# Later batches read x once and move its turned blocks inside SBUF; the first batch's softmax maximum is taken in two parts

## The chip, the cores and the metric

One core of a Trainium2 chip runs the whole program. The metric is the device time of one execution in microseconds (us). The engines are named as in the profile: PE (TensorE matmul) with PEld (its weight loads), DVE (VectorE), ACT (ScalarE), POOL (GpSimd) and SP (SyncE), whose queue issues the DMAs here.

## What is computed

Two rounds of attention over a small set of 32 inducing rows, then an FFN with a squared ReLU over all 49,920 rows:

```python
B, N, m, C = 4, 12480, 32, 128          # x: B x N x C, inducing: m x C, all float32
def mab(q, kv):                          # softmax attention, scale 1/sqrt(C)
    s = scale * (q @ kv.transpose(0, 2, 1))
    s = s - s.max(-1, keepdims=True)
    a = np.exp(s)
    a /= a.sum(-1, keepdims=True) + 1e-09
    return a @ kv
h = mab(I, x)                            # I: the inducing rows, for each batch
y = mab(x, h).reshape(B * N, C)
hidden = np.maximum(y @ w_in, 0.0)       # w_in: 128 x 2048
out = hidden * hidden @ w_out            # w_out: 2048 x 128
```

## The kernel before, in words

**Tiles.** A batch of 12,480 rows is cut into 26 lanes of 480 rows (LANE = 32 x 15), and the lanes into NG = 7 groups: six of four lanes and one of two. A group is a tile `xn` in SBUF (partition p holds 15 rows of 128 numbers) and, turned, a tile `xt` (the 128 channels on the partitions). One FFN block works on one lane: 104 blocks in all, each with 16 hidden slices in four quads.

**Order.** The program builds a list of tasks with `add(engine, ns, fn, due, needs, ...)`: an engine, a cost in ns, a due time, the tasks that it needs and the buffers that it takes or reads. `Plan.run` schedules the list with these costs: of the tasks that an engine could start now it takes the one with the earliest due time, and the instructions are emitted in that order. Each engine, and SP's queue, then works through its own order on the chip and waits wherever an operand is not there yet. T_MAIN is the planned start of the FFN blocks, BLOCK = 15,100 ns is one block's share; the other constants at the top (W_DUE, FIRST_DUE, MIX_DUE, S1_LEAD, HI_DUE and so on) set due times.

**First attention of batch 0** (`FirstBatch`). Seven tiles `xn` are loaded. For each group PE transposes it in 128x128 pieces (L671), ACT or DVE copies the result to `xt` (L254, a helper), PE makes the scores `sp` (L696), and DVE writes the row maximum into a column of `bare` (L702). The scores of the first four groups are copied to SBUF. When all seven maxima are there, L569 to L585 form the common maximum over groups and lanes (`mx`, `lanes`, `top`, `neg`), ACT takes the exponentials (`e`, L603), DVE turns them (`et`, L610), and PE sums `et` with `xn` into `nb` (L619).

**End of a batch's first attention** (`first_end`). From the sums and totals come `hT` (the attended rows, turned; copied by L254) and `hw`, the product of `hT` with w_in in four chunks of 512 columns: PE `wp` (L753), ACT copies the chunk (L757), DVE writes the remainder on half of the partitions (L762). An FFN quad needs its chunk of `hw`.

**Second attention** (`Second`). For a group PE makes `na` from `xt` and `hT` (L796); DVE and ACT do a softmax over 32 in `d` (L802 to L826); the result is turned (`a`), split into a high and a low part (`sw`), and four DMAs a lane spread it to `st` (L843), the FFN's input. The first lane of the program has a small version of its own (`mini`, tiles with `0m`), which ends with L873 and L877 in place of the DMAs.

**Weights.** w_in and w_out arrive as pairs of words and are put together on ACT and DVE (`weights`, L287 to L308, joined at L353 and L372), in four chunks each.

**FFN block.** h on PE (L942), ReLU and square on ACT (L949, L963), `hi` and `lo` on DVE (L968, L973), three products each on PE (L1027, one slice by L1017); in the first two blocks one product instead (L984). The result is turned (`ob`, L1048) and stored by four DMAs (L1054).

**First attention of batches 1 to 3** (`First`), beside the FFN blocks of the batch before: SP loads the group as `xn` (L411), and once more from DRAM in blocks: `xb`, one buffer for two lanes, eight DMAs of 60 KB in runs of 128 bytes (L440). One DVE transpose of 32x32 blocks writes `xb` to `xt` (L443), twice for a full group, once for the half one. `weigh` then makes the scores (L465), maximum, exponentials and sums (L472 to L534), with a running maximum: each group's `neg` is the smaller of its own and the one before, and sums are scaled by `fade`.

Of the kernel before, what the change touches and what calls it, by code (L numbers as in the profile page):

```python
# [162 lines left out]
def induced_attention_then_squared_relu_ffn(  # L163
# [232 lines left out]
    class First:  # L396
# [3 lines left out]
        def __init__(self, b, g, due, begun=None):  # L400
# [19 lines left out]
            for h in range(self.L // 2):  # L420
                self.turned.append(self.turn_blocks(h, due - 6000 + 3000 * h))
# [7 lines left out]
        def turn_blocks(self, h, due):  # L429
            b = self.b  # L430
            bb = Buffer("xb")
            v = {}

            def load():
                v["xb"] = xb_pool.tile([P, 2, NR, S], F32, tag="xb", name=f"xb_{self.n}_{h}")
                for l in range(2):
                    at = self.at + (2 * h + l) * LANE
                    rows = x[b, at:at + LANE, :].rearrange("(t r) (g c) -> g t r c", r=NR, c=S)
                    for c in range(P // S):
                        nc.sync.dma_start(v["xb"][c * S:(c + 1) * S, l], rows[c])  # L440

            def turn():
                nc.vector.transpose(  # L443
                    self.xt_tile()[:, 2 * h:2 * h + 2].rearrange("c l r t -> c (l r t)"),
                    v["xb"].rearrange("p l r c -> p (l r c)"),
                )
# [103 lines left out]
    class FirstBatch:  # L550


        def __init__(self, due, step, mix_due, mix_step):
            self.s = s = state.setdefault(0, {"xt": {}, "bxt": {}, "turned": {}})
            s["first"] = self
            self.sp, self.xn, self.bsp = {}, {}, {}
            self.loaded, self.tops, bxs = [], [], []
            v = {}
# [3 lines left out]
            kept = NG - 3  # L562

            for g in range(NG):
                self.group(g, due + step * g, g < kept, bare)

            def lanes():
                v["mx"] = tiny.tile([P, 1], F32, tag="mx", name="mx_0")
                nc.vector.tensor_reduce(v["mx"], bare[:, 0, :NG], axis=AX.X, op=ALU.max)  # L569

            def lanes2():
                v["lanes"] = tiny.tile([P, Q], F32, tag="lanes", name="lanes_0")
                nc.vector.tensor_scalar_mul(v["lanes"], lane_q, v["mx"])

            def gather():
                v["tops"] = self.last_sp[:, LANE:LANE + Q]
                nc.tensor.matmul(v["tops"], same, v["lanes"], start=True, stop=True)

            def most():
                v["top"] = tiny.tile([P, 1], F32, tag="top", name="top_0")  # L580
                nc.vector.tensor_reduce(v["top"], v["tops"], axis=AX.X, op=ALU.max)

            def shift():
                self.neg = tiny.tile([P, 1], F32, tag="neg", name="neg_0", bufs=4)
                nc.vector.tensor_scalar_mul(self.neg, v["top"], -scale)  # L585

            d = mix_due
            bg = self.bsp[NG - 1]
            t = add("DVE", 100, lanes, d - 3000, self.tops)
            t = add("DVE", 110, lanes2, d - 3000, [t])  # L590
            t = add("PE", 110, gather, d - 3000, [t], reads=[bg])
            t = add("DVE", 100, most, d - 3000, [t], reads=[bg])
            shifted = add("DVE", 70, shift, d - 3000, [t])
            bn = Buffer("s")
            powered, mixed = None, None
            for g in range(NG):
# [4 lines left out]
                def power(g=g, R=R, c=c):  # L601
# [3 lines left out]
                        bias=self.neg[:R], scale=scale, accum_out=bare[:R, 1, g:g + 1],  # L605
# [8 lines left out]
                def mix(g=g, R=R, c=c):  # L614
                    if g == 0:
                        v["nb"] = early_bank("nb_0")[:, :C]
                    for r in range(NR):
# [525 lines left out]
```

## Time and profile before

| | before |
|---|---|
| median of three runs | 1653.51 us (1652.34 to 1654.84) |
| the profiled execution | 1653.15 us, span 1651.4 us |
| busy PE / DVE / ACT / POOL | 1615.4 / 1535.6 / 1526.3 / 45.1 us |
| granted TensorE clock, mean | 0.993 |
| DMA | 101.30 MB in 389,085 packets, 368,848 of them under 512 B |
| HBM read / written | 48.94 / 25.56 MB |

In a row of the timeline stand start (us), duration (us), engine, source line, operation, output and inputs with shapes; "xN" merges N neighbours; a bracket gives the idle time before it and what ended it. "SPq" is SP's queue. A row of a group of instructions has count, then busy us and the mean in ns, then idle time before and what ended most of it. A row of DMA issues has the KB of one and the median us from issue to landing. A row of waits has total us, times and the longest.

### The profile page before, as it was taken

What the parts mean: (1) busy time and instruction counts of PE and PEld (TensorE: products, weight loads), DVE (VectorE), ACT (ScalarE), POOL (GpSimd) and SP (SyncE); (2) the same over time, 40 slices, a digit from 0 to 9 for tenths busy, and PEclk for the clock granted to TensorE, in tenths of its full rate; (3) what the DMA queues carried; (4) which work ended last, traced back from release to release, by engine and by line L of the source; (5) the groups of instructions that cost most, each with busy time, mean ns of one, the idle gap of its engine ahead of it and who ended that gap; (6) DMA issues with size and microseconds to landing.
All of it is one profiled execution on the core that took longest, in us unless ns stands there. A gap on an engine that the chain in (4) does not pass through costs nothing.

```text
span 1651.4 us, 22141 instructions
## 1 busy us (share of the span) xinstructions
PE 1615.4 (98%) x8004; PEld 1282.1 (78%) x8004; DVE 1535.6 (93%) x1457; ACT 1526.3 (92%) x1425; POOL 45.1 (3%) x39
## 2 busy tenths in 40 slices
PE   7889999999999999999999999999999999999998
PEld 5368787887778788888877778878787878888886
DVE  6759999999989999999999999999999999999997
ACT  5679999999989999999989999999999999999997
POOL 0000000000000000000000000000000000000000
PEclk9999999999999999999999999999999999999999
DMA  7441533422243333323233334233012212111211
GB/s 246 111 87 43 100 56 69 70 44 60 49 86 71 59 68 79 57 49 77 41 63 78 76 60 91 47 67 73 13 31 43 40 24 51 37 31 19 43 30 19
DMA packets 389085, 101.30 MB, mean 61 GB/s; under 512 B 368848, under 2 KB 385136, under 8 KB 388976
## 3 DMA queue, kind: packets, MB, share of 16 engines
q1 hardware_dynamic: 388976, 99.89, 29.8%
q8 instruction: 63, 1.03, 0.3%
q14 instruction: 46, 0.38, 0.1%
HBM read 48.94 MB, written 25.56 MB: 45 GB/s over the span
## 4 chain that ended last, share of the span: by engine, by line
PE 89%; DVE 5%; SPq 2%; issue 2%; DMA 1%; ACT 1%; DVEq 0%; POOL 0%; ACTq 0%
PE op L1027 57%; PE h L942 21%; PE op L1017 5%; DVE lo L973 2%; SPq L440 1%; PE nb L518 1%; PE na L796 1%; DVE hi L968 1%; PE sp L465 1%; PE op L984 1%; PE xtp L671 1%; SPq L843 1%; PE wp L753 1%; DVE hw L762 0%; DMA st<-sw 0%
## 5 line engine op out<-in xcount | busy, mean ns | idle before, releaser
L949 ACT ACTIVATE g<-h 128x960 f32<-128x960 f32 x832 | 780.4, 983 | 63.8 <-PE h L942 46.5
L973 DVE TENSOR_TENSOR lo<-g,hi 128x1920 fp32r<-128x1920 f32 (+1 forms) x409 | 823.7, 2015 | 15.2 <-DVE z L823 0.3
L963 ACT ACTIVATE g<-g 128x1920 f32<-128x1920 f32 (+1 forms) x419 | 760.2, 1814 | 4.5
L942 PE MATMUL h<-st,hw 128*128 128x480 f32 x1664 | 516.0, 392 | 6.4 <-DMA st<-sw 5.1
L968 DVE CAST hi<-g 128x1920 fp32r<-128x1920 f32 (+1 forms) x409 | 442.6, 1082 | 47.7 <-ACT g L963 39.7
L1027 PE MATMUL op<-hi,wo_hi 128*128 128x480 f32 x1530 | 442.5, 403 | 0.0
L1027 PE MATMUL op<-hi,wo_lo 128*128 128x480 f32 x1530 | 435.7, 383 | 0.0
L1027 PE MATMUL op<-lo,wo_hi 128*128 128x480 f32 x1530 | 415.4, 381 | 0.6 <-DVE lo L973 0.6
L942 PEld LDWEIGHTS h<-st,hw 128*128 128x128 f32 x1664 | 309.0, 188 | 93.9 <-issue 28.2
L1027 PEld LDWEIGHTS op<-hi,wo_hi 128*128 128x128 f32 x1530 | 286.2, 188 | 81.4 <-issue 36.6
L1027 PEld LDWEIGHTS op<-lo,wo_hi 128*128 128x128 f32 x1530 | 286.6, 188 | 54.8 <-issue 5.9
L1027 PEld LDWEIGHTS op<-hi,wo_lo 128*128 128x128 f32 x1530 | 287.2, 188 | 49.1 <-issue 3.0
L1017 PE MATMUL op<-g,wo_whole 128*128 128x480 f32 x204 | 98.9, 566 | 0.0
L820 POOL TENSOR_SCALAR z<-z 128x15 f32<-128x15 f32 (+1 forms) x28 | 44.0, 1571 | 1535.8 <-DVE z L816 1453.3
L1048 DVE STREAM_TRANSPOSE ob<-op 128x480 f32<-128x480 f32 (+1 forms) x105 | 70.3, 670 | 3.2 <-PE op L1027 2.9
L443 DVE STREAM_TRANSPOSE xt<-xb 128x960 f32<-128x960 f32 x39 | 45.2, 1159 | 14.3 <-DMA xb<-in_x_dram 11.3
L1017 PEld LDWEIGHTS op<-g,wo_whole 128*128 128x128 f32 x204 | 38.3, 189 | 7.5 <-issue 1.6
L518 PE MATMUL nb<-xn,et 128*32 128x128 f32 (+1 forms) x630 | 23.4, 282 | 5.7 <-DVE et L510 5.7
L518 PEld LDWEIGHTS nb<-xn,et 128*32 128x32 f32 (+1 forms) x630 | 17.5, 112 | 13.0 <-DVE et L510 6.5
L796 PE MATMUL na<-xt,hT 128*32 128x480 f32 (+1 forms) x224 | 26.9, 551 | 0.0
L465 PE MATMUL sp<-xt,indT 128*32 128x480 f32 x156 | 22.5, 578 | 2.2 <-DVE xt L443 2.2
L254 ACT CAST sw<-a 128x480 fp32r<-128x480 f32 (+1 forms) x25 | 14.2, 570 | 8.9 <-DVE a L830 8.8
(132 smaller groups left out, 469.7 us busy)
## 6 DMA issues: line engine op xcount, KB each, us to landing
out_dram<-ob SPq DMA_DIRECT2D x412, 60.0 KB, 2.2
xn<-in_x_dram SPq DMA_DIRECT2D x24, 960.0 KB, 5.1
st<-sw SPq DMA_DIRECT2D x380, 60.0 KB, 2.0
xb<-in_x_dram SPq DMA_DIRECT2D x312, 60.0 KB, 2.6
xn<-in_x_dram SPq DMA_DIRECT2D x4, 480.0 KB, 5.1
hi_i<-in_moe_w_in_dram SPq DMA_DIRECT2D x2, 512.0 KB, 14.5
lo_i<-in_moe_w_in_dram SPq DMA_DIRECT2D x2, 512.0 KB, 17.4
hi_o<-in_moe_w_out_dram SPq DMA_DIRECT2D x2, 512.0 KB, 4.3
```

Of the source, the lines that this page charges most:

```text
L443: nc.vector.transpose(self.xt_tile()[:, 2 * h:2 * h + 2].rearrange("c l r t -> c (l r t)"), v["xb"].rearrange("p l r c -> p (l r c)"),)
L518: nc.tensor.matmul(v["nb"][c * M:(c + 1) * M, :], self.et[:R, r, :], self.xn[:R, r, :], start=r < Q, stop=r >= NR - Q,)
L796: nc.tensor.matmul(v["na"][i * M:(i + 1) * M, :W], s["hT"][:, :M], cols[:, c:c + W], start=True, stop=True,)
L820: E.tensor_scalar(v["z"], v["z"], 1e-9, 0.0, ALU.add, ALU.add)
L942: nc.tensor.matmul(c["hp"][:, l, :LANE], s["hw"][:, f * P:(f + 1) * P], second.st[k], start=True, stop=True,)
L949: nc.scalar.activation(v["g"][:, 2 * i:2 * i + 2, :], c["hp"][:, :, :LANE], AF.Relu)
L963: nc.scalar.activation(v["g"][:, h], v["g"][:, h], AF.Square)
L968: nc.vector.tensor_copy(v["hi"][:, h], v["g"][:, h])
L973: nc.vector.tensor_sub(v["lo"][:, h], v["g"][:, h], v["hi"][:, h])
L1017: nc.tensor.matmul(w["op"][:, :LANE], wo_whole, v["g"][:, 3, :], start=False, stop=False)
L1027: nc.tensor.matmul(w["op"][:, :LANE], pools["wo"][wo][:, 4 * j + l, :], v[name][:, l, :], start=(j == x_ == 0 and l == 0), stop=(j == NQ - ...
L1048: nc.vector.transpose(w["ob"][:, rows].rearrange("p r c -> p (r c)"), w["op"][:, rows.start * S:rows.stop * S])
```

## The change

Four things change.

1. In `First`, `xb` is no longer loaded. DVE transposes the 32x32 blocks of `xn` into `xb` (two channel blocks at a time, so two transposes for each group, also for the half one), and DMAs inside SBUF move rows of 1920 bytes from `xb` to `xt`: for a full group eight for each half. The transpose waits for `xn` and a free `xb`; the move takes the place in `xt`; the scores wait for the moves.
2. `FirstBatch` takes its maximum in two parts: groups 0 to 4 (KEPT = 5, their scores are copied to SBUF) and groups 5 and 6. The second part uses the running maximum, a `fade`, and its own `nb`.
3. `first_end` uses the small PSUM pool for chunks 1 to 3 of `wp` in batch 0. The gates in GATES change: chunks 1 to 3 of `wp` wait until the first lane's `st` is ready (before: until its softmax is normed), and the copy of chunk 0 waits for the exponential of the small softmax.
4. T_MAIN and many due times have other values.

The diff, with the parts left out that only hand indices on:

```diff
@@ -183,21 +183,22 @@
     scale = 1.0 / math.sqrt(C)
 
     GB, HB, LB, OB, MB, STB, XTB, XNB, XBB = 3, 2, 2, 2, 2, 6, 7, 2, 1
-    T_MAIN, BLOCK = 42100.0, 15100.0
+    T_MAIN, BLOCK = 48100.0, 15100.0
     ORDER = "x0 x1 x2 x3 i0 x4 x5 x6 i1 i2 i3 o0 o1 o2 o3".split()
-    W_DUE = [11900.0, 21100.0, 24900.0, 30200.0, 41500.0, 46000.0, 50000.0, 53300.0]
-    FIRST_DUE, FIRST_STEP, MIX_DUE, MIX_STEP, MINI_DUE = 6000.0, 2600.0, 25000.0, -1000.0, -800.0
-    S2_LEAD, S2_LEAD_0, S2_STEP, S1_LEAD, S1_STEP = 44500.0, 26000.0, 1600.0, 11100.0, 3000.0
+    W_DUE = [20000.0, 26800.0, 31000.0, 33000.0, 39500.0, 46500.0, 50000.0, 53600.0]
+    FIRST_DUE, FIRST_STEP, MIX_DUE, MIX_STEP, MINI_DUE = 5800.0, 3100.0, 24500.0, 700.0, -1000.0
+    S2_LEAD, S2_LEAD_0, S2_STEP, S1_LEAD, S1_STEP = 44500.0, 30000.0, 1600.0, 10700.0, 3000.0
     WHOLE = lambda b, g, k: True
     PLAIN = lambda b, g, k: b == g == 0 and k < 2
     GATES = lambda s, m: dict(
-        s0=m.ready[0], s1=m.ready[0], s2=m.ready[0], s3=m.ready[0], w0_1=m.normed, w0_2=m.normed, w0_3=m.normed,
+        s0=m.ready[0], s1=m.ready[0], s2=m.ready[0], s3=m.ready[0], w0_1=m.ready[0], w0_2=m.ready[0], w0_3=m.ready[0], p0_0=m.powered,
         o1=m.normed, o2=m.normed, o3=m.normed,
     )
-    SPLIT_DUE, SPLIT_STEP, PLAIN_DUE = 64000.0, 0.0, 9500.0
+    KEPT = 5
+    SPLIT_DUE, SPLIT_STEP, PLAIN_DUE = 65000.0, 200.0, 11500.0
     FIRST_PAIRS, LAST_PAIRS = 2, 1
-    G1_DUE, SQ_DUE, HI_DUE, LO_DUE, OP_DUE = -1500.0, 6000.0, 2500.0, 6500.0, 10300.0
-    OT_DUE = 7900.0
+    G1_DUE, SQ_DUE, HI_DUE, LO_DUE, OP_DUE = -1500.0, 5700.0, 6500.0, 5500.0, 14100.0
+    OT_DUE = 5900.0
     LATE_RELU, LATE_HI, LATE_G1, LATE_OT = 250.0, 50.0, 250.0, 400.0
     PATIENCE = (20000.0, 60000.0, 40.0)
 
@@ -417,8 +418,8 @@
-            for h in range(self.L // 2):
-                self.turned.append(self.turn_blocks(h, due - 6000 + 3000 * h))
+            for h in range(2):
+                self.turned.append(self.turn_blocks(h, due - 8000 + 4000 * h))
@@ -427,28 +428,28 @@
             return self.s["xt"][self.g]
 
         def turn_blocks(self, h, due):
-            b = self.b
+            R = self.rows
             bb = Buffer("xb")
             v = {}
 
-            def load():
+            def turn():
                 v["xb"] = xb_pool.tile([P, 2, NR, S], F32, tag="xb", name=f"xb_{self.n}_{h}")
-                for l in range(2):
-                    at = self.at + (2 * h + l) * LANE
-                    rows = x[b, at:at + LANE, :].rearrange("(t r) (g c) -> g t r c", r=NR, c=S)
-                    for c in range(P // S):
-                        nc.sync.dma_start(v["xb"][c * S:(c + 1) * S, l], rows[c])
-
-            def turn():
                 nc.vector.transpose(
-                    self.xt_tile()[:, 2 * h:2 * h + 2].rearrange("c l r t -> c (l r t)"),
-                    v["xb"].rearrange("p l r c -> p (l r c)"),
+                    v["xb"][:R].rearrange("p j r t -> p r j t"),
+                    self.xn[:R, :, 2 * h * S:2 * (h + 1) * S].rearrange("p r (j c) -> p r j c", j=2),
                 )
 
-            t = state["blocks"] = add("SP", 2050, load, due - 20000, [state.get("blocks"), self.begun], takes=[bb], late=0)
-            t = state["turn"] = add("DVE", 1090, turn, due, [t, state.get("turn"), self.begun],
-                                    takes=[] if h else [self.bt], reads=[bb] + ([self.bt] if h else []))
-            return t
+            def move():
+                xt = self.xt_tile()
+                for j in range(2):
+                    c0 = (2 * h + j) * S
+                    for q in range(self.L):
+                        nc.sync.dma_start(xt[c0:c0 + S, q], v["xb"][q * M:(q + 1) * M, j])
+
+            t = state["turn"] = add("DVE", 1090, turn, due, [self.loaded, state.get("turn"), self.begun],
+                                    takes=[bb], reads=[self.bx])
+            return add("SP", 150 * self.L, move, due, [t], late=0, takes=[] if h else [self.bt],
+                       reads=[bb] + ([self.bt] if h else []))
 
         def weigh(self, due, step):
             s, n, L, R = self.s, self.n, self.L, self.rows
@@ -553,47 +554,58 @@
...
+            self.kept = kept = KEPT
             for g in range(NG):
+                self.group(g, due + step * g, bare)
+            prev = None
+            for i, span in enumerate([range(kept), range(kept, NG)]):
+                prev = self.part(i, span, prev, bare, [mix_due - kept * mix_step, mix_due][i], mix_step)
+
+        def part(self, i, span, prev, bare, due, step):
+            v, new = {}, {}
+            last = span[-1]
+
+            def most_of():
+                v["mx"] = tiny.tile([P, 1], F32, tag="mx", name=f"mx_0_{i}")
+                nc.vector.tensor_reduce(v["mx"], bare[:, 0, span.start:span.stop], axis=AX.X, op=ALU.max)
 
             def lanes():
+                v["lanes"] = tiny.tile([P, Q], F32, tag="lanes", name=f"lanes_0_{i}")
                 nc.vector.tensor_scalar_mul(v["lanes"], lane_q, v["mx"])
 
             def gather():
+                v["tops"] = self.bank[last][:, LANE:LANE + Q]
                 nc.tensor.matmul(v["tops"], same, v["lanes"], start=True, stop=True)
 
             def most():
+                v["top"] = tiny.tile([P, 1], F32, tag="top", name=f"top_0_{i}")
                 nc.vector.tensor_reduce(v["top"], v["tops"], axis=AX.X, op=ALU.max)
 
             def shift():
+                new["neg"] = tiny.tile([P, 1], F32, tag="neg", name=f"neg_0_{i}", bufs=4)
+                if prev:
+                    nc.vector.scalar_tensor_tensor(new["neg"], v["top"], -scale, prev["neg"], ALU.mult, ALU.min)
+                else:
+                    nc.vector.tensor_scalar_mul(new["neg"], v["top"], -scale)
+
+            def fade():
+                v["fade"] = tiny.tile([P, 1], F32, tag="fade", name="fade_0")
+                nc.scalar.activation(v["fade"], prev["neg"], AF.Exp, bias=new["neg"], scale=-1.0)
+
+            bg = self.bs[last]
+            t = add("DVE", 100, most_of, due - 3000, [self.tops[g] for g in span])
+            t = add("DVE", 110, lanes, due - 3000, [t])
+            t = add("PE", 110, gather, due - 3000, [t], reads=[bg])
+            t = add("DVE", 100, most, due - 3000, [t], reads=[bg])
+            shifted = new["shifted"] = add("DVE", 70, shift, due - 3000, [t, prev and prev["shifted"]])
             bn = Buffer("s")
+            powered, mixed = prev and prev["powered"], prev and prev["mixed"]
+            for g in span:
                 R = M * lanes_of[g]
                 c = {}
                 be, bet = Buffer("e"), Buffer("et")
@@ -602,7 +614,7 @@
-                        bias=self.neg[:R], scale=scale, accum_out=bare[:R, 1, g:g + 1],
+                        bias=new["neg"][:R], scale=scale, accum_out=bare[:R, 1, g:g + 1],
@@ -612,41 +624,49 @@
...
+                        v["nb"] = early_bank(f"nb_0_{i}")[:, :C]
+                            start=g == span[0] and r < Q, stop=g == last and r >= NR - Q,
+                d = due + step * (g - span[0])
+                powered = add("ACT", 820, power, d, [shifted, powered, self.kept_at.get(g)], takes=[be], reads=[self.bsp[g]])
+                mixed = add("PE", 950, mix, d + 2000, [t, mixed], mode="n", takes=[bn] if g == span[0] else [],
+                            reads=[bet, self.bxs[g]] + ([] if g == span[0] else [bn]))
+            new["powered"], new["mixed"] = powered, mixed
+                new["acc"] = att.tile([P, C], F32, tag="hacc", name=f"hacc_0_{i}")
+                if prev:
+                    nc.vector.scalar_tensor_tensor(new["acc"], prev["acc"], v["fade"], v["nb"], ALU.mult, ALU.add)
+                else:
+                    copy(new["summed"], new["acc"], v["nb"])
+                self.acc = new["acc"]
+                new["z"] = tiny.tile([P, 1], F32, tag="z", name=f"z_0_{i}")
+                nc.vector.tensor_reduce(new["z"], bare[:, 1, span.start:span.stop], axis=AX.X, op=ALU.add)
+                self.sum = new["z"]
+                if prev:
+                    self.sum = tiny.tile([P, 1], F32, tag="zs", name="zs_0")
+                    nc.vector.scalar_tensor_tensor(self.sum, prev["z"], v["fade"], new["z"], ALU.mult, ALU.add)
+
+            f = add("ACT", 250, fade, due, [shifted]) if prev else None
+            d = due + step * len(span)
+            self.totalled = new["totalled"] = add("DVE", 250 if prev else 100, add_z, d, [powered, f, prev and prev["totalled"]])
+            self.summed = new["summed"] = add("DVE", 260, add_h, d + 1000, [mixed, f, prev and prev["summed"]], reads=[bn])
+            return new
+
+        def group(self, g, due, bare):
...
@@ -706,12 +726,12 @@
-            self.tops.append(add("DVE", wide_ns(LANE), top, due + 2000, [t], reads=[bs]))
-            if kept:
+            self.tops[g] = add("DVE", wide_ns(LANE), top, due + 2000, [t], reads=[bs])
+            if g < self.kept:
-                self.tops.append(c["keep"])
+                self.kept_at[g] = c["keep"]
@@ -746,7 +766,7 @@
-            if b:
+            if b or k:
@@ -771,10 +791,10 @@
-            bw = Buffer("m" if b else "h")
+            bw = Buffer("m" if b or k else "h")
-            t = add("ACT", 520, lambda k=k: part(k), d, [t], reads=[bw])
+            t = w_gate[f"p{b}_{k}"] = add("ACT", 520, lambda k=k: part(k), d, [t], reads=[bw])
@@ -886,7 +906,7 @@
-            t = add("ACT", wide_ns(W, "ACT"), power, d + 3 * step, [t], reads=[bd])
+            t = self.powered = add("ACT", wide_ns(W, "ACT"), power, d + 3 * step, [t], reads=[bd])

```

More of the change, by code (lines that the diff above doesn't have):

```diff
@@ L555, in __init__ @@
             s["first"] = self
-            self.sp, self.xn, self.bsp = {}, {}, {}
-            self.loaded, self.tops, bxs = [], [], []
-            v = {}
+            self.sp, self.xn, self.bsp, self.bank, self.bs, self.bxs = {}, {}, {}, {}, {}, {}
+            self.loaded, self.tops, self.kept_at = [], {}, {}
             bare = const.tile([P, 2, 8], F32, name="bare")
@@ L561, in __init__ @@
             nc.gpsimd.memset(bare[:, 1], 0.0)
-            kept = NG - 3
+            self.kept = kept = KEPT
             for g in range(NG):
-                self.group(g, due + step * g, g < kept, bare)
+                self.group(g, due + step * g, bare)
[8 more added lines that the diff above has]
+                nc.vector.tensor_reduce(v["mx"], bare[:, 0, span.start:span.stop], axis=AX.X, op=ALU.max)
@@ L567, in lanes @@
             def lanes():
[L568 to L572, printed above, removed]
+                v["lanes"] = tiny.tile([P, Q], F32, tag="lanes", name=f"lanes_0_{i}")
                 nc.vector.tensor_scalar_mul(v["lanes"], lane_q, v["mx"])
             def gather():
-                v["tops"] = self.last_sp[:, LANE:LANE + Q]
+                v["tops"] = self.bank[last][:, LANE:LANE + Q]
@@ L577, in gather @@
                 nc.tensor.matmul(v["tops"], same, v["lanes"], start=True, stop=True)
             def most():
-                v["top"] = tiny.tile([P, 1], F32, tag="top", name="top_0")
+                v["top"] = tiny.tile([P, 1], F32, tag="top", name=f"top_0_{i}")
                 nc.vector.tensor_reduce(v["top"], v["tops"], axis=AX.X, op=ALU.max)
             def shift():
-                self.neg = tiny.tile([P, 1], F32, tag="neg", name="neg_0", bufs=4)
-                nc.vector.tensor_scalar_mul(self.neg, v["top"], -scale)
@@ L587, in __init__ @@
[L587 to L593, printed above, removed]
+                new["neg"] = tiny.tile([P, 1], F32, tag="neg", name=f"neg_0_{i}", bufs=4)
[3 more added lines that the diff above has]
+                    nc.vector.tensor_scalar_mul(new["neg"], v["top"], -scale)
@@ L594, in __init__ @@
+            shifted = new["shifted"] = add("DVE", 70, shift, due - 3000, [t, prev and prev["shifted"]])
             bn = Buffer("s")
-            powered, mixed = None, None
-            for g in range(NG):
+            powered, mixed = prev and prev["powered"], prev and prev["mixed"]
+            for g in span:
                 R = M * lanes_of[g]
@@ L614, in mix @@
                 def mix(g=g, R=R, c=c):
-                    if g == 0:
-                        v["nb"] = early_bank("nb_0")[:, :C]
+                    if g == span[0]:
+                        v["nb"] = early_bank(f"nb_0_{i}")[:, :C]
                     for r in range(NR):
@@ L620, in mix @@
                             v["nb"][k * M:(k + 1) * M, :], c["et"][:R, r, :], self.xn[g][:R, r, :],
-                            start=g == 0 and r < Q, stop=g == NG - 1 and r >= NR - Q,
+                            start=g == span[0] and r < Q, stop=g == last and r >= NR - Q,
                         )
-                d = mix_due + mix_step * g
-                powered = add("ACT", 820, power, d, [shifted, powered], takes=[be], reads=[self.bsp[g]])
+                d = due + step * (g - span[0])
@@ L626, in __init__ @@
+                powered = add("ACT", 820, power, d, [shifted, powered, self.kept_at.get(g)], takes=[be], reads=[self.bsp[g]])
                 t = add("DVE", wide_ns(LANE), turn_e, d + 1000, [powered], takes=[bet], reads=[be])
-                mixed = add("PE", 950, mix, d + 2000, [t, mixed], mode="n", takes=[] if g else [bn],
-                            reads=[bet, self.bx[g]] + ([bn] if g else []))
+                mixed = add("PE", 950, mix, d + 2000, [t, mixed], mode="n", takes=[bn] if g == span[0] else [],
+                            reads=[bet, self.bxs[g]] + ([] if g == span[0] else [bn]))
@@ L630, in add_h @@
+            new["powered"], new["mixed"] = powered, mixed
             def add_h():
-                self.acc = att.tile([P, C], F32, tag="hacc", name="hacc_0")
-                copy(self.summed, self.acc, v["nb"])
-            def add_z():
-                self.sum = tiny.tile([P, 1], F32, tag="zs", name="zs_0")
-                nc.vector.tensor_reduce(self.sum, bare[:, 1, :NG], axis=AX.X, op=ALU.add)
-            self.totalled = add("DVE", 100, add_z, d + 2000, [powered])
-            self.summed = add("DVE", 210, add_h, d + 3000, [mixed], reads=[bn])
@@ L641, in induced_attention_then_squared_relu_ffn @@
-        bx = property(lambda self: self.bxs)
-        def group(self, g, due, kept, bare):
+                new["acc"] = att.tile([P, C], F32, tag="hacc", name=f"hacc_0_{i}")
[4 more added lines that the diff above has]
+                self.acc = new["acc"]
+            def add_z():
+                new["z"] = tiny.tile([P, 1], F32, tag="z", name=f"z_0_{i}")
[4 more added lines that the diff above has]
+                    nc.vector.scalar_tensor_tensor(self.sum, prev["z"], v["fade"], new["z"], ALU.mult, ALU.add)
@@ L688, in group @@
                 turned_.append(v["task"])
-            bs = Buffer("s")
+            bs = self.bs[g] = Buffer("s")
             c = {}
@@ L693, in score @@
                 c["sp"] = early_bank(f"sp_0_{g}")
-                self.sp[g], self.last_sp = c["sp"][:R, :LANE], c["sp"]
+                self.sp[g], self.bank[g] = c["sp"][:R, :LANE], c["sp"]
                 for q in range(L):
```

2 lines of the change are left out of this document (removed).

## The prediction

> **What bounds the kernel now.** I read the page's busy shares and chain first, then the busy time by stage, then who PE waits for after the start, then the timeline of the first 110 us.
>
> ```profile
> PE 1615.4 (98%) x8004; PEld 1282.1 (78%) x8004; DVE 1535.6 (93%) x1457; ACT 1526.3 (92%) x1425; POOL 45.1 (3%) x39
> PE 89%; DVE 5%; SPq 2%; issue 2%; DMA 1%; ACT 1%; DVEq 0%; POOL 0%; ACTq 0%
> ...
> 20.00:30.00 10.00, 8.13 (x67) 4.05 (x65) 9.47 (x18) 7.14 (x11) 0.00 (x0) 1.00 0.72 217
> 30.00:40.00 10.00, 6.35 (x123) 5.57 (x123) 8.69 (x21) 5.17 (x14) 0.00 (x0) 0.66 0.36 107
> 40.00:50.00 10.00, 8.60 (x109) 4.67 (x108) 7.42 (x22) 3.38 (x7) 0.00 (x0) 0.83 0.78 206
> 50.00:60.00 10.00, 7.44 (x29) 3.14 (x28) 9.79 (x21) 7.08 (x10) 0.86 (x1) 1.00 0.25 96
> 60.00:70.00 10.00, 9.33 (x33) 3.92 (x32) 7.40 (x14) 10.00 (x11) 0.15 (x1) 1.00 0.33 55
> 70.00:100.00 30.00, 22.55 (x88) 12.82 (x89) 13.03 (x23) 17.86 (x21) 0.29 (x1) 0.89 0.49 105
> ...
> 400.00:800.00 400.00, 397.23 (x1978) 317.33 (x1978) 383.87 (x359) 375.66 (x350) 12.32 (x8) 1.00 0.33 65
> ...
> PE h L942 <- DMA st<-sw: 5.1, 2, 2.8
> PE op L1027 <- DVE lo L973: 0.6, 2, 0.4
> ```
>
> The stage rows give window, length, then busy us of PE, weight load, DVE, ACT and POOL, granted clock, DMA share, GB/s. From 400 to 800 us PE is busy 397.23 of 400; the last two rows are all that PE matmuls wait for between 110 and 1640 us (5.1 + 0.6 us). So after about 105 us the time is PE's own work, which the change does not touch. It can gain only in the first 105 us, and it can lose anywhere. In those 105 us PE is not the bound: DVE is (9.47 of 10 in 20 to 30 us, 9.79 in 50 to 60), then the queue that issues DMAs.
>
> **The change, part one: the first batch's maximum in two parts.** Before, no exponential starts until all seven tiles have their maximum:
>
> ```profile
> 24.26 0.66 DVE L702 TENSOR_REDUCE bare<-sp 128x1 f32<-128x480 f32 x1
> 29.28 0.64 DVE L702 TENSOR_REDUCE bare<-sp 64x1 f32<-64x480 f32 x1
> 31.72 0.14 DVE L585 TENSOR_SCALAR neg<-top 128x1 f32<-128x1 f32 x1
> 31.95 0.69 ACT L603 ACTIVATE e<-sk,neg 128x480 f32<-128x480 f32 x1 [2.28 <-DVE neg L585]
> 39.98 0.66 ACT L603 ACTIVATE e<-sp,neg 64x480 f32<-64x480 f32 x1 [0.71 <-DVE et L610]
> 42.34 1.07 PE L619 MATMUL nb<-xn,et 64*32 64x128 f32 x30
> 44.74 0.29 DVE L254 COPY hT<-htp 128x128 f32<-128x128 f32 x1
> ```
>
> The fifth tile's maximum ends at 24.92, the seventh's at 29.92. From there to the first exponential is 2.03 us (31.95 - 29.92); the seven run at a pace of (39.98 - 31.95)/6 = 1.34 us; from the last one's start to the end of hT is 45.03 - 39.98 = 5.05 us. After the change the first five can start at 24.92 + 2.03 = 26.95 and take 5 x 1.34 = 6.7 us, to 33.65; the sixth starts there (its own maximum is ready at 31.95), the seventh at 34.99. hT then ends at 34.99 + 5.05 = 40.04, that is 5.0 us earlier. If the first five are quicker and the sixth starts at 31.95, it is 6.7 us. The added work (a second reduction, lanes, gather, shift, a 128x1 exponential, two joins) is some ten instructions of 0.14 to 0.4 us; only those of the second part are on the path, and they replace the same ones. I take 5.0.
>
> **Part two: the gates after hT.** The small softmax for the first block runs from hT to the first FFN matmul:
>
> ```profile
> 46.33 0.29 DVE L809 TENSOR_TENSOR d_0m<-d_0m,mx_0m 128x128 f32<-128x128 f32 x1
> 47.65 0.59 ACT L757 CAST hw<-wp 128x512 fp32r<-128x512 f32 x1 [3.71 <-PE wp L753]
> 48.13 0.31 ACT L812 ACTIVATE d_0m<-d_0m 128x128 f32<-128x128 f32 x1
> 52.32 1.30 DVE L762 TENSOR_TENSOR hw<-wp,hw 64x512 fp32r<-64x512 f32 x2
> 53.65 0.26 DVE L877 CAST st<-ap_0m 128x96 fp32r<-128x96 f32 x1
> 53.97 0.70 PE L942 MATMUL h<-st,hw 128*128 128x480 f32 x2
> ```
>
> Its input is ready at 46.62, but its exponential starts at 48.13, because ACT's queue has a copy (L757) first that waits for PE. The gate on p0_0 turns that order round: with 0.2 us for the handover, 48.13 - 46.62 - 0.2 = 1.3 us. The gates on w0_1 to w0_3 move two halves of hw (L762, 1.30 us) behind L877: another 1.3 us. What is late next: hw's other chunks then start after the first block has its softmax, and each needs PE, ACT and DVE once more before its quad. Together 5.0 + 2.6 = 7.6 us earlier for the first FFN matmul.
>
> **Part three: what DVE gives back.** The weights' work (w_in's and w_out's reconstruction on DVE) is all still there, only due later. It ends with this instruction:
>
> ```profile
> 71.57 0.65 DVE L372 TENSOR_TENSOR lo_o<-lo_o 128x512 f32<-128x512 f32 x1
> ```
>
> The first FFN block needs it for its last quad. DVE's idle time from 20 to 70 us is 0.53 + 1.31 + 2.58 + 0.21 + 2.60 = 7.2 us by the stage rows, so this end can't move by more than 7.2 us however the work is ordered; the new small instructions take about 0.7 of it. So the start gains 6.5 us, not 7.6. Ends: 0 (the idle time stays, merely moved) and 7.2.
>
> **Part four: x loaded once.** Removed: 312 loads of 60 KB in 128-byte runs. Added: 312 moves of 60 KB (16 per full tile, as before), so the issue queue has as much to do. Three more transposes (42 for 39, since the half tile now takes two of 64 partitions).
>
> ```profile
> L443 DVE STREAM_TRANSPOSE xt<-xb 128x960 f32<-128x960 f32 x39 | 45.2, 1159 | 14.3 <-DMA xb<-in_x_dram 11.3
> st<-sw SPq DMA_DIRECT2D x380, 60.0 KB, 2.0
> xb<-in_x_dram SPq DMA_DIRECT2D x312, 60.0 KB, 2.6
> ```
>
> Three times 1.16 = 3.5 us of DVE lie in the time in which PE is the bound and waits 0.6 us for DVE: nothing, unless DVE, 383.87 of 400 busy, falls behind; then at most 3.5. A strided transpose is not in the trace; I take the same 1.16 us, and the bound is twice that, 49 us of DVE over the whole run, which its 4% idle just holds. The lighter DMA traffic (18.7 of 101.3 MB in short runs now stays in SBUF, in long rows) frees nothing that PE waits for.
>
> What the moves change is the order of waits. Before, the data waits for the load, then the transpose goes straight into xt and the score follows. After, the transpose needs only the tile that is loaded anyway, but the score (L465 on PE) waits for eight moves, and the second half's transpose waits until the first half's moves have left the single xb buffer. At the start the old order costs this:
>
> ```profile
> 63.03 5.24 SPq L440 DMA_DIRECT2D xb<-in_x_dram  x8
> 68.38 7.54 SPq L843 DMA_DIRECT2D st<-sw  x12
> 72.62 1.78 PE L942 MATMUL h<-st,hw 128*128 128x480 f32 x4
> 84.72 1.18 DVE L443 STREAM_TRANSPOSE xt<-xb 128x960 f32<-128x960 f32 x1 [6.73 <-DMA xb<-in_x_dram]
> 87.08 1.93 PE L518 MATMUL nb<-xn,et 128*32 128x128 f32 x30 [5.75 <-DVE et L510]
> ```
>
> DVE sits 6.73 us on a block load that the issue queue brought late, the transpose of e is behind it, and PE idles 5.75 us. That wait can't come back in this form. But the queue is as full (eight issues take 5.24 us, so 0.66 each, and st's three spreads of 7.54 us stand behind them), and the moves wait there for DVE. Bounds: 5.75 us gained; or 8 us lost, one move's passage (5.24 + 2.0) and a handover, if PE's score gets the place of DVE's wait. I take 0: the wait changes its place.
>
> In the later groups the rows to go by are these:
>
> ```profile
> 668.01 1.14 DVE L443 STREAM_TRANSPOSE xt<-xb 128x960 f32<-128x960 f32 x1
> 669.18 5.92 SPq L440 DMA_DIRECT2D xb<-in_x_dram  x8
> 685.28 1.17 DVE L443 STREAM_TRANSPOSE xt<-xb 128x960 f32<-128x960 f32 x1
> 686.48 5.28 SPq L440 DMA_DIRECT2D xb<-in_x_dram  x8
> 688.96 1.01 PE L465 MATMUL sp<-xt,indT 128*32 128x480 f32 x8
> ```
>
> The first half is transposed 21 us before the score, the second 3.7 us before it, with a due time of 3 us before it. The new due times are 8 and 4 us before it, so by the same offset the second goes 4.7 us ahead. A transpose then needs 1.17 + 5.3 + 2.0 = 8.5 us until its eight moves have landed: 3.8 us too late, less some 0.8 us that PE's first three score matmuls cover, 3.0 us. The kernel's plan books only 0.6 us for the eight issues. Against it: the transposes no longer wait for a load or for xt's place, the tile is there some 30 us ahead, and DVE's gaps may take both early, as they took the first half here. I take 0, with the other end as a rival.
>
> The Trainium skill, SBUF — State Buffer, sections "Door 1: The DMA port swizzle" and "The DMA setup-cost knee", speaks against the move: 32 partitions reach 8 of 16 ports (about 218 GB/s) behind a fixed cost of some 2 us, which by an estimate from that page makes 2.3 us for 60 KB. The row of st<-sw, a transfer of the same shape, has 2.0, so the measurement decides; by the page the rival below would be 0.3 us a group dearer.
>
> **Sum.** 5.0 + 2.6, cut by DVE to 6.5, and 0 for part four: -6.5 us. The profiled execution took 1653.15 us (span 1651.4), 0.4 under the median 1653.51; 1653.51 - 6.5 = 1647.0.
>
> **Rivals.** (a) The start is faster and the 5.75 us stall goes as well: 1647.0 - 5.75 = 1641. For it: DVE no longer waits for a late load. Against: the issue queue is as full.
> (b) The gain at the start is given back: the first block still waits for the weights on DVE (71.57) and for st in the issue queue: 1653.5, no change. For it: DVE has 9.79 of 10 busy there. Against: 7.2 us idle before it.
> (c) Slower: PE's score stands in its queue for the moves. 3.0 us in each of 18 full tiles and about 1 in three half ones: 57 us, 1704. From (6.5 + 3.3)/3.0, four tiles on, it decides the sign; at eight tiles it is 1647 + 24 = 1671. For it: the second half's transpose ran 3.7 us ahead though its data had landed (669.18 + 5.92 + 2.6 = 677.7) 7.6 us earlier. Against: the first half ran 21 us ahead.
>
> **How the numbers follow.** A repeat of this kernel tells about 0.2%, 3.3 us, from no change. Forecast 0.50 (its own range 1643 to 1650), (a) 0.14, (b) 0.13, (c) 0.23. So faster 0.64, same 0.13, slower 0.23. The range 1638 to 1664 leaves out about 0.05 below and 0.15 of (c) above.
>
> **What would show it.** hT ending near 40 us and the first L942 near 46 to 47; the last L372 near 65; no DVE wait for xb near 85; PE over 99% busy from 110 us on. Wrong, if PE's score or DVE's transposes show waits of 2 us or more for the moves in every group, or if the first FFN block still ends at the same time.

## The result and the profile after

| | before | after |
|---|---|---|
| median of four runs | 1652.92 us | 1710.12 us |
| ratio after / before | | 1.034 (95% interval 1.032 to 1.036) |
| profiled span | 1651.4 us | 1709.7 us |

The forecast was 1647.0 us, faster; the kernel became 57 us slower, near the 1704 us of rival (c). The loss comes from the moves, as (c) has it, but not by the wait that (c) names.

First the page of the kernel after: busy shares, chain, the transposes, the score, the moves.

```profile
PE 1638.1 (96%) x8006; PEld 1292.1 (76%) x8006; DVE 1540.4 (90%) x1470; ACT 1528.7 (89%) x1424; POOL 47.4 (3%) x39
...
PE 77%; DVE 8%; SPq 5%; DMA 4%; issue 3%; ACT 2%; DVEq 0%; ACTq 0%
...
L437 DVE STREAM_TRANSPOSE xb<-xn 128x960 f32<-128x960 f32 (+1 forms) x42 | 49.3, 1173 | 68.0 <-DMA xt<-xb 59.7
...
L466 PE MATMUL sp<-xt,indT 128*32 128x480 f32 x156 | 26.4, 599 | 6.4 <-DMA xt<-xb 6.4
...
xt<-xb SPq DMA_DIRECT2D x312, 60.0 KB, 2.0
```

PE's share of the chain falls from 89% to 77%; SP's queue rises from 2% to 5%, DMA from 1% to 4%, DVE from 5% to 8%. DVE stands 59.7 us, in 17 waits, in front of the new transposes (L437) until a move of an earlier half has landed. PE's own wait in front of the score is 6.4 us, once (8.7 us with its weight loads). The transposes themselves cost what was expected: 1173 ns, 42 of them.

The stages, first of the kernel before, then after (window, length, busy us and number of records of PE, weight load, DVE, ACT, POOL, then clock, DMA share, GB/s):

```profile
50.00:110.00 60.00, 49.32 (x183) 26.20 (x183) 36.64 (x63) 44.42 (x47) 1.30 (x2) 0.94 0.43 93
110.00:1250.00 1140.00, 1134.46 (x5658) 906.53 (x5657) 1092.98 (x1021) 1076.48 (x1001) 31.84 (x23) 1.00 0.31 61
1250.00:1640.00 390.00, 389.83 (x1760) 321.20 (x1760) 370.67 (x298) 380.81 (x339) 11.14 (x6) 1.00 0.19 35
```

```profile
50.00:110.00 60.00, 49.28 (x160) 24.83 (x159) 32.83 (x55) 42.08 (x45) 0.97 (x2) 0.83 0.38 99
110.00:1250.00 1140.00, 1102.19 (x5391) 874.24 (x5390) 1045.39 (x972) 1026.79 (x948) 29.47 (x21) 0.98 0.28 60
1250.00:1640.00 390.00, 390.00 (x1782) 318.31 (x1781) 371.50 (x317) 377.79 (x342) 16.21 (x8) 1.00 0.19 34
```

From 110 to 1250 us, where the tiles of batches 1 to 3 are prepared, PE does 267 fewer of its 5658 matmuls. At 5658/1140 = 4.96 per us that is 54 us, almost the whole loss. After 1250 us, where no tile is left to turn, both run alike.

Not all of the loss is idle time of PE. The span grew by 58.3 us, and 22.7 us of that is PE's own busy time, 1638.1 us against 1615.4 for as many matmuls (8006 and 8004 records). The granted clock was lower, 0.979 in the mean against 0.993. Around the stall shown next:

```profile
455.00:460.00 5.00, 2.95 (x10) 1.51 (x9) 0.00 (x0) 1.17 (x2) 0.00 (x0) 1.00 0.38 87
460.00:465.00 5.00, 1.33 (x3) 0.82 (x3) 3.76 (x5) 0.66 (x2) 0.00 (x0) 0.82 0.20 48
465.00:470.00 5.00, 5.00 (x18) 3.53 (x18) 4.88 (x7) 4.49 (x5) 0.32 (x1) 0.84 0.28 65
470.00:475.00 5.00, 5.00 (x25) 4.30 (x24) 4.91 (x6) 5.00 (x7) 0.00 (x0) 1.00 0.05 12
```

From 465 to 470 us PE is busy throughout, but at a clock of 0.84, and at 1.00 only from 470 on: here the cost of the stall goes on after PE's wait has ended. Over the run the same 1664 matmuls of `h` take 399 ns in the mean instead of 392. That the lower clock makes up the whole 22.7 us fits these figures, but no run tests it alone.

One stall in the timeline of the kernel after:

```profile
452.91 1.01 PE L816 MATMUL na<-xt,hT 128*32 128x480 f32 x8
453.98 13.34 SPq L447 DMA_DIRECT2D xt<-xb  x16
454.16 0.68 DVE L822 STREAM_TRANSPOSE d<-na 128x480 f32<-128x480 f32 x1
456.98 0.97 PE L1037 MATMUL op<-g,wo_whole 128*128 128x480 f32 x2
461.18 1.18 DVE L437 STREAM_TRANSPOSE xb<-xn 128x960 f32<-128x960 f32 x1 [6.34 <-DMA xt<-xb]
463.67 2.08 PE L773 MATMUL wp<-w_in_sb,hT 128*128 128x512 f32 x2 [5.72 <-DVE hw L782]
464.22 2.15 DVE L993 TENSOR_TENSOR lo<-g,hi 128x1920 fp32r<-128x1920 f32 x1
464.34 0.60 ACT L832 ACTIVATE d<-d 128x480 f32<-128x480 f32 x1 [7.44 <-DVE d L829]
```

The first half was turned at 407.76, long before; its move waits until PE has read the old tile in that place of `xt` (L816). At 453.98 its eight issues begin (the row merges them with the second half's eight). The plan books 0.6 us for the eight and frees `xb` 0.1 us later, so in DVE's order the second transpose comes next but one. DVE reaches it at 454.84 (454.16 + 0.68) and stands for 6.34 us; everything behind it stands too, FFN work among it; ACT idles 7.44 us and PE 5.72. This is one of the 17 waits.

### The profile page after: what moved, and what is told of

Read it like the earlier page. It is cut to its first block, busy times and chain, and to the rows that moved or that the text cites. A ratio compares the mean times of both kernels' runs of the same rounds, so it can differ in the third digit from the quotient of the medians.

```text
span 1709.7 us, 22177 instructions
## 1 busy us (share of the span) xinstructions
PE 1638.1 (96%) x8006; PEld 1292.1 (76%) x8006; DVE 1540.4 (90%) x1470; ACT 1528.7 (89%) x1424; POOL 47.4 (3%) x39
## 3 DMA queue, kind: packets, MB, share of 16 engines
HBM read 29.77 MB, written 25.56 MB: 32 GB/s over the span
## 4 chain that ended last, share of the span: by engine, by line
PE 77%; DVE 8%; SPq 5%; DMA 4%; issue 3%; ACT 2%; DVEq 0%; ACTq 0%
PE op L1047 50%; PE h L962 18%; SPq L447 4%; PE op L1037 4%; DMA xt<-xb 3%; DVE lo L993 2%; DVE hi L988 2%; ACT g L969 1%; PE nb L519 1%; DVE xb L437 1%; DMA lo_i<-in_moe_w_in_dram 1%; PE na L816 1%; PE sp L466 1%; PE op L1004 1%; PE wp L773 1%
## 5 line engine op out<-in xcount | busy, mean ns | idle before, releaser
L962 PE MATMUL h<-st,hw 128*128 128x480 f32 x1664 | 527.5, 399 | 3.3 <-ACT g L969 3.3
L1047 PE MATMUL op<-hi,wo_hi 128*128 128x480 f32 x1530 | 450.2, 403 | 11.9 <-DVE hi L988 11.9
L1047 PE MATMUL op<-lo,wo_hi 128*128 128x480 f32 x1530 | 431.7, 385 | 11.9 <-DVE lo L993 11.9
L1047 PE MATMUL op<-hi,wo_lo 128*128 128x480 f32 x1530 | 425.9, 383 | 0.0
L962 PEld LDWEIGHTS h<-st,hw 128*128 128x128 f32 x1664 | 313.3, 190 | 97.4 <-issue 34.8
L437 DVE STREAM_TRANSPOSE xb<-xn 128x960 f32<-128x960 f32 (+1 forms) x42 | 49.3, 1173 | 68.0 <-DMA xt<-xb 59.7
L840 POOL TENSOR_SCALAR z<-z 128x15 f32<-128x15 f32 (+1 forms) x28 | 46.4, 1656 | 1581.3 <-DVE z L836 1581.3
L466 PE MATMUL sp<-xt,indT 128*32 128x480 f32 x156 | 26.4, 599 | 6.4 <-DMA xt<-xb 6.4
L832 ACT ACTIVATE d<-d 128x480 f32<-128x480 f32 (+1 forms) x28 | 16.5, 591 | 16.7 <-DVE d L829 16.7
L773 PE MATMUL wp<-w_in_sb,hT 128*128 128x512 f32 x32 | 20.6, 737 | 10.9 <-DVE hw L782 10.7
L519 PE MATMUL nb<-xn,et 128*32 128x128 f32 (+1 forms) x630 | 23.4, 282 | 3.8 <-DVE et L511 3.8
```

Source lines behind the costliest of these rows:

```text
L437: nc.vector.transpose(v["xb"][:R].rearrange("p j r t -> p r j t"), self.xn[:R, :, 2 * h * S:2 * (h + 1) * S].rearrange("p r (j c) -> p r j ...
L466: nc.tensor.matmul(v["sp"][q * M:(q + 1) * M, :LANE], indT, s["xt"][self.g][:, q].rearrange("c r t -> c (r t)"), start=True, stop=True,)
L840: E.tensor_scalar(v["z"], v["z"], 1e-9, 0.0, ALU.add, ALU.add)
L962: nc.tensor.matmul(c["hp"][:, l, :LANE], s["hw"][:, f * P:(f + 1) * P], second.st[k], start=True, stop=True,)
L1047: nc.tensor.matmul(w["op"][:, :LANE], pools["wo"][wo][:, 4 * j + l, :], v[name][:, l, :], start=(j == x_ == 0 and l == 0), stop=(j == NQ - ...
```

## The experiments

Three theories. T: DVE's place in its own order, behind a move in flight, costs the time. R1: the moves' passage through the issue queue costs it, wherever it is waited for. R2: the new FFN due times leave PE without work. Each ratio is to runs of the kernel before that were taken beside the experiment (their medians: 1653.06 us for 1 to 4, 1653.85 for 5 to 8, 1652.25 for 9 to 12), with its 95% interval. In the diffs `...` stands for lines and arguments that do not bear on the point.

**1. Two xb buffers.**

```diff
-XTB, XNB, XBB = 7, 2, 1
+XTB, XNB, XBB = 7, 2, 2
-add("SP", 150 * self.L, move, due, [t], ...)
+add("SP", 150 * self.L, move, due, [t] + self.turned, ...)
...
-v["sk"] = att.tile([P, NB, 2, 2, M], F32R, tag="sk", ...)
+whole = att.tile([P, 2, LANE], F32R, tag="sw", ...)
...
```

> The changed kernel with two xb buffers instead of one (the room comes from a small tile of the first block that shares another's place; the second half's moves are ordered behind the first half's). Theory T: what costs the 57 us is DVE standing in its own order, 17 times, 59.7 us in all, until the first half's moves have left the single xb buffer. With two buffers these waits of L437 fall from 59.7 to under 10 us and the time to 1645 to 1662 us. Rival R1: the moves' passage through the issue queue is what costs, wherever it is waited for; then the wait passes to PE's score (now 8.7 us) and the time stays at 1690 or more. Rival R2: the new due times of the FFN (hi, lo, products) leave PE without work; then nothing changes, 1700 to 1715.

Measured: 1668.03 us, ratio 1.008 (1.007 to 1.010). Three quarters of the loss are gone with one more buffer, and PE's wait in front of the score does not take its place (4.0 us); R1 as stated and R2 as the whole cause fall. But T's numbers were missed: 31.6 us of DVE's waits remain, and the time is 6 us above its range.

```profile
600.06 1.01 PE L816 MATMUL na<-xt,hT 128*32 128x480 f32 x8
...
603.24 10.07 SPq L447 DMA_DIRECT2D xt<-xb  x16
609.75 1.18 DVE L437 STREAM_TRANSPOSE xb<-xn 128x960 f32<-128x960 f32 x1 [7.58 <-DMA xt<-xb]
```

In these rows of its timeline both buffers have been full since 549 us and wait for one place in `xt`; after L816 all 16 issues go out, and now it is the third transpose that stands behind them.

**2. The old loads, all else as changed.** `turn_blocks` and its due times as in the kernel before.

```diff
-self.turned.append(self.turn_blocks(h, due - 8000 + 4000 * h))
+self.turned.append(self.turn_blocks(h, due - 6000 + 3000 * h))   # with load() from DRAM
```

> The changed kernel with the xb loads from DRAM and the transposes as before (part four undone; maximum in two parts, gates and due times as changed). T and R1: the loss is gone, 1645 to 1656 us; what is left against 1653 is the worth of the start, which the changed kernel's trace puts near 0 (first FFN matmul 1.75 us earlier, second block's end 2.6 us later). R2: still 1690 or more.

Measured: 1650.38 us, 0.998 (0.997 to 0.999). Without part four the loss is gone, so it sits there. What remains of the change is worth 2.7 us (1653.06 - 1650.38).

**3. The moves alone on the kernel before.**

```diff
-self.turned.append(self.turn_blocks(h, due - 6000 + 3000 * h))   # with load() from DRAM
+self.turned.append(self.turn_blocks(h, due - 8000 + 4000 * h))   # with move() in SBUF
```

> The kernel before with part four alone (x loaded once, transposes from xn, moves; due times of the two transposes 8 and 4 us ahead), everything else as before. T and R1: 1690 to 1715 us, DVE's waits for xt<-xb 40 us or more. R2: 1645 to 1658 us.

Measured: 1737.84 us, 1.050 (1.049 to 1.052): the direction of T and R1, but 23 us beyond the range. Here PE waits for the score as well (all waits of the run; us, times, longest):

```profile
DVE xb L436 <- DMA xt<-xb: 52.7, 12, 5.7
...
PEld sp L465 <- DMA xt<-xb: 26.9, 27, 5.7
...
PE sp L465 <- DMA xt<-xb: 25.7, 9, 7.2
```

So both waits exist: the one of rival (c) on PE and the one on DVE. How large each is depends on the other due times.

**4. The plan told the moves' real cost**, one buffer.

```diff
-add("SP", 150 * self.L, move, ...)
+add("SP", 1300 * self.L, move, ...)
-at = max(at, u.end + 100.0 + t.late)
+at = max(at, u.end + (2100.0 if b.tag == "xb" and u.by == "SP" else 100.0) + t.late)
```

> The changed kernel, single xb buffer, but the plan is told what the trace shows: eight issues occupy the queue for 5.2 us (before: 0.6 us booked), and xb comes free 2.1 us after the last issue (before: 0.1 us). Only the order of instructions changes. T: the second transpose is placed some 8 us behind the first with FFN work between, its waits fall under 10 us, and the time to 1648 to 1665 us. R1: the same direction, since the score too is placed later, but the issue queue's work remains: 1660 to 1690. R2: 1700 or more.

Measured: 1654.24 us, 1.000 (0.999 to 1.001). The same instructions, the same moves, the same single buffer: only their order differs, and the loss is gone. This is inside T's range and under R1's. Waits for the moves that are left:

```profile
PEld sp L466 <- DMA xt<-xb: 12.3, 9, 5.2
...
PE sp L466 <- DMA xt<-xb: 9.0, 4, 4.8
...
DVE xb L437 <- DMA xt<-xb: 8.0, 3, 4.9
```

**5. Both cures.** The edits of 1 and 4 together.

> The changed kernel with both: two xb buffers, and the plan told the moves' real occupation of the queue (5.2 us for eight) and of xb (2.1 us more). T (DVE's place in its own order behind a move in flight is what costs, and each of the two cures left a rest: 31.6 us of waits with two buffers, 8.0 us with the true costs): the waits fall under 5 us, the time to 1644 to 1651 us, under the kernel with the old loads (1650.4). R1 (the queue itself): no better than the better of the two, 1653 to 1660.

Measured: 1651.51 us, 0.998 (0.998 to 0.999); DVE's waits for the moves 1.6 us. The waits are as T expects, the time half a microsecond above its range; no better than the old loads of 2, which have the same ratio.

**6. Both cures, old gates.**

```diff
-w0_1=m.ready[0], w0_2=m.ready[0], w0_3=m.ready[0], p0_0=m.powered,
+w0_1=m.normed, w0_2=m.normed, w0_3=m.normed,
```

> As the run before, with the gates of the kernel before (wp's chunks 1 to 3 after the small softmax is normed, no gate on the copy of chunk 0). In the changed kernel four wp products stand in PE's queue ahead of the first FFN matmul (49.43 to 53.2 us). If the gates cost the start what the earlier hT gave it, the first FFN matmul comes 1 to 3 us earlier and the time falls by as much; if the gates help as the prediction had it, it rises by up to 2.6 us; no difference over 1 us speaks for DVE's weights as the bound of the start.

Measured: 1650.57 us, 0.998 (0.997 to 0.999): no difference to 5, though the first FFN matmul comes 1.4 us later (53.59 against 52.17). The expectation would read that as DVE's weights being the bound, but their last join (L373) comes later too, at 69.73 against 67.42, and the time does not follow it.

**7. Old loads, old gates.** The edit of 6 on experiment 2.

> The changed kernel with the old loads (1650.4) and the old gates: what is left of the change is the maximum in two parts and the due times. The same three readings as in the run before: 1 to 3 us less, up to 2.6 us more, or no difference.

Measured: 1654.24 us, 1.000 (1.000 to 1.002). Here the gates are worth some 3 to 4 us: 3.9 by the two medians (1654.24 - 1650.38), 3.1 when each is set against the kernel before beside it. The first FFN matmul starts at 54.71 against 51.32 in 2. With 6 this leaves the gates' worth open: it depends on what else stands in the queues at the start. And what is left without the gates (the maximum in two parts, the PSUM pool and the due times) brings no measurable gain: `hT` ends at 41.59, 3.4 us earlier than before, but the first FFN matmul comes 0.7 us later than before.

**8. The moves from POOL's queue**, one buffer, costs as changed.

```diff
-nc.sync.dma_start(xt[c0:c0 + S, q], v["xb"][q * M:(q + 1) * M, j])
+nc.gpsimd.dma_start(xt[c0:c0 + S, q], v["xb"][q * M:(q + 1) * M, j])
...
-return add("SP", 150 * self.L, move, ...)
+return add("POOL", 150 * self.L, move, ...)
```

> The changed kernel, single buffer, with the moves issued from POOL's queue instead of SP's. R1's strong form (the moves wait behind stores and spreads in SP's queue): the passage is shorter, DVE's waits fall from 59.7 to under 30 us, the time under 1690. T: the passage is the eight issues' own time and one landing, on any queue; the waits stay at 45 us or more and the time at 1695 or more, longer if POOL takes longer for an issue than the 0.6 us of SP.

Measured: 1671.78 us, 1.011 (1.009 to 1.012). Between the two readings: under R1's 1690, with 37.7 us of waits above its 30. So T was too narrow. One wait is 2.5 us in the mean here (37.7 in 15) and 3.5 in the kernel after (59.7 in 17), and eight issues are 0.7 us shorter by the medians below, so a shorter passage accounts for most of that. How much of the time it accounts for is open: the plan now has the move in POOL's order, and DVE's order comes out different too. The issues, SP's in the kernel after and POOL's here (ns, least/median/most):

```profile
L447 SPq DMA_DIRECT2D xt<-xb x312: 507/588/1752, 59.5 to 1249.7; - x156
```

```profile
L447 POOL DMA_DIRECT2D xt<-xb x312: 496/496/1383, 59.8 to 1212.3; - x156
```

**9. Only the issue time corrected.** Of the two corrections in 4, the cost alone.

> The changed kernel, single buffer, the plan told only that eight moves occupy the queue for 5.2 us (before: 0.6), not that xb stays taken for another 2 us. If the booked issue time is the whole of the error, 1651 to 1658 us as with both corrections (1654.2); if the landing counts as well, each close pair of transposes still waits about 2 us: 15 pairs, 30 us of DVE, 1665 to 1685.

Measured: 1667.11 us, 1.009 (1.008 to 1.011). The booked issue time alone wins 43 of the 56 us that experiment 4 wins; the 2 us until xb is free win 13 more. The time is in the second reading's range, but not by the waits that it names: DVE waits 12.8 us for moves, in 7 waits, not 30 in 15, and once 8.7 us for a load of `xn`. How the last 13 us arise stays open.

**10. The FFN's due times as before.**

```diff
-G1_DUE, SQ_DUE, HI_DUE, LO_DUE, OP_DUE = -1500.0, 5700.0, 6500.0, 5500.0, 14100.0
+G1_DUE, SQ_DUE, HI_DUE, LO_DUE, OP_DUE = -1500.0, 6000.0, 2500.0, 6500.0, 10300.0
```

and OT_DUE, SPLIT_DUE, SPLIT_STEP and PLAIN_DUE as before.

> The changed kernel with the FFN's own due times (square, hi, lo, products, store) as before. The kernel before with the moves alone took 1738, the whole change 1710: if the new FFN due times soften the stall (they let the products run one quad later behind hi and lo, so PE has more in hand while DVE stands), this takes 1725 to 1745; if they have no part in it, 1705 to 1715.

Measured: 1732.95 us, 1.049 (1.048 to 1.051). With DVE's waits about the same (62.8 us against 59.7) the time is 23 us longer, so the new due times do not cause the loss, they lessen it; R2 had their sign wrong. PE's waits fit: from 110 us on it waits 36.7 us for `hi` and `lo`, against 23.8 in the kernel after, and in front of the score 17.6 us in all against 6.4.

**11. Old loads, two xb buffers.** The buffer of 1 on experiment 2.

> The changed kernel with the old loads (1650.4) and two xb buffers. DVE's waits for late block loads there are 20.0 us, 14.1 of them before 115 us. If they still cost the start, two buffers take most of them away and the time falls to 1643 to 1649; if PE is covered anyway, it stays at 1649 to 1652.

Measured: 1643.17 us, 0.995 (0.993 to 0.996): 9.1 us under the kernel before (1652.25 beside it). The first two rows are experiment 2's, the others are this run's (waits before 115 us, and its timeline):

```profile
DVE xt L444 <- DMA xb<-in_x_dram: 14.1, 3, 9.0
...
PE nb L519 <- DVE et L511: 7.6, 1, 7.6
```

```profile
DVE xt L444 <- DMA xb<-in_x_dram: 7.8, 1, 7.8
...
72.48 0.68 DVE L511 STREAM_TRANSPOSE et<-e 128x480 f32<-128x480 f32 x1 [2.15 <-ACT e L501]
...
77.29 1.07 PE L519 MATMUL nb<-xn,et 128*32 128x128 f32 x30
81.48 1.18 DVE L444 STREAM_TRANSPOSE xt<-xb 128x960 f32<-128x960 f32 x1 [7.79 <-DMA xb<-in_x_dram]
```

One late load is left, and now `et` (L511) is ahead of it in DVE's order: PE no longer idles in front of L519, where experiment 2 still lost 7.6 us. Two buffers on the kernel before, without the rest of the change, were not run.

**12. Old loads at their real cost**, one buffer (5.3 us booked for 2.05).

```diff
-t = state["blocks"] = add("SP", 2050, load, ...)
+t = state["blocks"] = add("SP", 5300, load, ...)
```

> The changed kernel with the old loads, one buffer, the plan told that eight loads occupy the queue for 5.3 us (before: 2.05). The same reading as for two buffers: 1643 to 1649 if the late loads cost the start, 1649 to 1652 if not; over 1655 if the st spreads, which stand behind these loads, come later by the new order.

Measured: 1647.0 us, 0.997 (0.996 to 0.998), inside the first reading: 5.3 us under the kernel before beside it, where experiment 2 was 2.7 under its own. So one number of the plan is worth some 2.6 us here as well.

## Why the prediction was wrong, step by step

**Part four, "I take 0, with the other end as a rival", is the step that failed.** It put at nothing a wait that it had priced on PE alone: the score 3.0 us late in each of 18 full tiles, about 1 in three half ones. The runs show another place. PE waits 6.4 us for moves, DVE 59.7 us, and all that stands behind DVE waits too. The prediction named DVE's waits only as a sign of being wrong and gave them no price. It wrote down the condition (the second half's transpose waits until the first half's moves have left the single xb buffer) and the number that decides it (the plan books 0.6 us for eight issues), but did not put them together: a plan that believes `xb` free after 0.7 us sets the second transpose right behind the first half's move, wherever that move is held up by `xt`'s place. The row that spoke for 0, the first half turned 21 us before the score, says nothing of the second. With the chance of 0.23 for (c) the forecast lay on the wrong side; that (c)'s 57 us came out was luck, since its wait is not the one measured. Experiments 4 and 9 show the cause: with both figures of the plan corrected and nothing else, DVE's waits go from 59.7 to 8.0 us and the loss against the kernel before from 57 us to nothing measurable. Against the old loads (2) the moves are still some 4 us behind.

**Transposes at 1.16 us: right.** Strided ones take 1.17 us. **Lighter traffic frees nothing: borne out.** HBM reads fall from 48.94 to 29.77 MB (19.2 MB, not 18.7: the profile's KB is 1024 bytes), and experiment 2, which loads x twice, is no slower than 5.

**Moves' landing at 2.0 us: right.** The Trainium skill, SBUF — State Buffer, sections "Door 1: The DMA port swizzle" and "The DMA setup-cost knee", gave 2.3 us by an estimate; the moves' own row has 2.0, so the trace differs and decides.

**Part one, hT 5.0 us earlier: mis-sized by 1.2 us.**

```profile
35.82 0.64 ACT L615 ACTIVATE e<-sp,neg 64x480 f32<-64x480 f32 x1
40.90 0.29 DVE L255 COPY hT<-htp 128x128 f32<-128x128 f32 x1
```

The last exponential starts at 35.82 (predicted 34.99), hT ends at 41.19 (predicted 40.04, before 45.03): 3.8 us. In experiment 2 it ends at 40.29, so the size is not the same in every order.

**Part two, first FFN matmul at 46.4: wrong.**

```profile
43.69 0.31 ACT L832 ACTIVATE d_0m<-d_0m 128x128 f32<-128x128 f32 x1 [4.05 <-DVE d_0m L829]
49.43 3.78 PE L773 MATMUL wp<-w_in_sb,hT 128*128 128x512 f32 x4
49.89 0.26 DVE L897 CAST st<-ap_0m 128x96 fp32r<-128x96 f32 x1 [0.21 <-ACT st L893]
52.22 2.10 PE L962 MATMUL h<-st,hw 128*128 128x480 f32 x4
```

The exponential goes ahead of the copy as predicted. But from hT's end to the end of L897 it takes 50.15 - 41.19 = 8.96 us, against 53.91 - 45.03 = 8.88 before: DVE does some 6 us of the weights' work in that stretch, between the instructions of the small softmax, where it did 2 before. And four of the products that the gates move now stand in PE's queue right ahead of the first FFN matmul. It comes at 52.22, 1.75 us earlier instead of 7.6. The gates themselves work the way that was forecast: without them it comes later, by 1.4 us in 6 and 3.4 us in 7, for 2.6 forecast. What the sum missed is that the weights' work set back by the due times lands on the path behind hT.

**Part three, the weights' end near 65: wrong in the kernel after, and not shown as the bound.**

```profile
66.05 1.18 DVE L437 STREAM_TRANSPOSE xb<-xn 128x960 f32<-128x960 f32 x1 [5.80 <-DMA xt<-xb]
76.05 0.68 DVE L373 TENSOR_TENSOR lo_o<-lo_o 128x512 f32<-128x512 f32 x1
```

The last weight join (L373) comes at 76.05, 4.5 us later than before (71.57), behind one of DVE's waits for a move. In experiment 2, without the moves, it comes at 68.85, 2.7 us earlier, which is also the whole gain of that kernel. This fits DVE as the bound of the start, but the two do not always go together: in 11 it comes 4.2 us earlier (67.34) and the gain is 9.1 us, and from 5 to 6 it moves by 2.3 us and the time does not follow.

**Rival (a): its stall was real, but not removed by the change.** In experiment 2 PE still idles 7.6 us there. The stall goes in 11, with two `xb` buffers and the old loads. That run is 9.1 us under the kernel before, where (a) had summed 12.3 (6.5 + 5.75).

## What to carry to other kernels

Where an order is fixed ahead by a plan, a step that moves to a DMA queue must be booked with its issue time (here about 0.6 us for each DMA) and with the landing before its buffer is free again; the figures stand in the trace (here 588 ns and 2.0 us). Look for what the plan will set right behind such a step on an engine that is 93% busy: the wait shows up there, not where the data is used. And try a second buffer before a new data path: here, on the old loads with the rest of the change, it was worth more than the new path.

## What had not been expected of the hardware

An issue takes nearly the same on SP's queue whether it moves 32 rows of 1920 bytes inside SBUF (588 ns, median) or loads 480 runs of 128 bytes from DRAM (623 ns in the kernel before), so larger runs hardly relieved the queue. From POOL's queue, which has no other DMAs here, the same moves took 496 ns each (median) and 1.9 us to land; DVE's busy time stayed as it was (1539.3 us against 1540.4).
